# Fewer VectorE operations for the constants, and w_out as pairs of rows: a fused Nystrom attention and feed-forward kernel

## The chip, the cores and the metric

The kernel runs on one core of a Trainium2 chip. The metric is the device time of one execution in microseconds. A core has TensorE (PE in the profile; its weight loads are listed apart as PEld), VectorE (DVE), ScalarE (ACT), GpSimd (POOL) and SyncE (SP), each with its own queue of instructions that it takes in order, and 16 DMA engines that all queues share. Two notions matter below. A matmul has a loaded operand (the weights, put into TensorE by a weight load) and a moving operand that streams past it. And a group of TensorE results lies in PSUM until another engine copies it out.

## The reference

For 8 batches of 8 heads, 576 positions and 64 dimensions, the attention is Nystrom's: landmarks are means over groups of 18 positions, three softmax matrices are made with them, and the middle one is inverted by six iterations. The result goes through a feed-forward layer without a nonlinearity:

```python
A = sm(q, k_lm); Bm = sm(q_lm, k_lm); C = sm(q_lm, k)
Z = Bm.transpose(0, 1, 3, 2) / (norm1 * norminf + 1e-06)
for _ in range(6):
    Z = 2 * Z - Z @ Bm @ Z
x = A @ Z @ C @ v              # then (tokens, heads * dim): 4608 x 512
a = x @ w1                     # 512 x 1024
b = x @ w2
h = a * b @ w3                 # 1024 x 1024
out = h @ w_out                # 1024 x 512
```

All inputs and the output are fp32. Since nothing stands between w3 and w_out, the kernel multiplies these two first.

## The kernel before

All instructions are in an order written out by hand: each engine runs its own in the order in which the program states them. The string ORDER (line 32) lists the steps after the opening; a word such as `TK0.1` names a step and a batch, and `F` is one step of the fold.

The **opening** (lines 580 to 615) issues the first loads on the SyncE and ScalarE queues, starts some idle matmuls on TensorE (`warm_up`), has GpSimd copy one element of a late w_out block (`gate`, line 603) so that the q and k loads issued after it on GpSimd's queue wait for that block, issues those four loads and the loads of w1 and w2 (`load_weight`), builds the constants on VectorE (`constants`, line 162), and takes the first step of the fold.

The **fold** (line 505) makes w34 = w3 @ w_out, 1024 x 512. For precision each factor is split in two fp16 parts, a high and a low one, after a scaling by 256, and three of the four products are summed. `split(c)` does that for a block of 128 rows of w_out: ScalarE makes the high part, VectorE the low part. `turn(j, cc)` turns half a block of w3: TensorE transposes four pieces of 128 x 128 (line 517, moving operand the identity, loaded operand the piece of w3f) into a PSUM tile `big`, then ScalarE and VectorE split it into `w3t` (lines 522 and 523). `product(j, c)` is three matmuls of 512 columns into one accumulator (line 530); after eight of them ScalarE copies the block of w34 out (line 533). `before` and `order` in `fold` say which split and which turn stand ahead of which product: 64 products, 16 turns and 8 splits. After the first steps, blocks of w3 are used in turn out of three buffers, and the attention's first steps stand between the steps of the fold.

The **attention** of a batch takes q and k through 32 x 32 transposes on VectorE (`TK`, `TQ`, line 143), sums landmarks (`SK`, `SQ`), and makes scores (lines 248, 274, 322) from the tile `lm`, in which neighbouring landmarks of one head pair lie eight fp16 apart. The inverse runs in six steps (`I`, line 399). Constants are used there: `mask4` in the norms and in the inverse, `eye`, `eye2`, `bt`, `onesq` in the denominators (line 362), `selc` in the normalisation (line 382). Then `project` (`G`, line 442), `up` (`U`, line 455) and `down` (`W`, line 495) do the feed-forward layer.

Of the kernel before, what the change touches and what calls it, by code (L numbers as in the profile page):

```python
# [14 lines left out]
B = 8  # L15
H = 8
S = 576
D = 64
# [10 lines left out]
WS = 256.0  # L29
CHAINS = ((0,), (1, 2), (3, 4), (5, 6), (7,))  # L30

ORDER = """
F F F F F F F F F F F F F TK0.0 F F F F F TQ0.0 TQ1.0 F F L3.3 F TK1.0 F F F F F SK0.0 SK1.0 F F
SQ0.0 P.4 F F F F L3.5 F L3.7 F F TQ0.1 TK0.1 SQ1.0 F F L3.6 TK1.1 F E.0 F B.0 F C0.0 SK0.1 N.0
F F F A0.0 R.0 FV.0 TQ1.1 F SK1.1 F I0.0 F F D.0 I1.0 F I2.0 Y0.0 Y1.0 SQ0.1 Y2.0 LK0.2 F X.0 F
I3.0 LK1.2 F F F I4.0 V0.0 V1.0 SQ1.1 LQ0.2 LQ1.2 E.1 F LK0.3 TK0.2 TK1.2 F LK1.3 I5.0 F V2.0
LV0.2 F TQ0.2 TQ1.2 A0.1 Z.0 SK0.2 LV0.1 LV1.1 F M0.0 LV2.1 F LV3.1 D.1 Y0.1 Y1.1 Y2.1 G0.0 G1.0
G2.0 M1.0 SK1.2 F SQ0.2 TK0.3 G3.0 TK1.3 C0.1 X.1 F F F F U0a.0 U0b.0 U1a.0 U1b.0 U2a.0 U2b.0
LQ0.3 TQ0.3 LQ1.3 LK0.4 U3a.0 LV1.2 V0.1 U3b.0 SQ1.2 E.2 U4a.0 U4b.0 B.1 U5a.0 U5b.0 N.1 V1.1
SK0.3 V2.1 R.1 U6a.0 U6b.0 TQ1.3 U7a.0 I0.1 M0.1 LK1.4 LQ0.4 U7b.0 W0.0 SK1.3 I1.1 W1.0 I2.1  # L40
A0.2 LV2.2 TK0.4 LV3.2 W0.1 I3.1 TK1.4 W1.1 I4.1 M1.1 LQ1.4 W0.2 TQ0.4 I5.1 W1.2 SQ0.3 SQ1.3
TQ1.4 Z.1 SK0.4 E.3 SK1.4 SQ0.4 LV0.3 C0.2 G0.1 D.2 G1.1 G2.1 W0.3 Y0.2 G3.1 V0.2 V1.2 Y1.2 V2.2
LV0.4 Y2.2 U0a.1 U0b.1 LV1.3 LK0.5 U1a.1 U1b.1 LV1.4 LK1.5 X.2 U2a.1 U2b.1 U3a.1 U3b.1 Z.2 SQ1.4
E.4 U4a.1 U4b.1 U5a.1 G0.2 TK0.5 U5b.1 U6a.1 U6b.1 M0.2 LQ0.5 LQ1.5 W1.3 U7a.1 LV2.3 U7b.1 LV3.3
M1.2 W0.4 G1.2 G2.2 G3.2 B.3 TK1.5 W1.4 U0a.2 A0.3 W0.5 U0b.2 U1a.2 LV2.4 D.3 Y0.3 Y1.3 SK0.5
U1b.2 Y2.3 C0.3 W1.5 LK0.6 U2a.2 U2b.2 U3a.2 W0.6 X.3 U3b.2 U4a.2 N.3 SK1.5 V0.3 V1.3 V2.3 R.3
U4b.2 TK0.6 W1.6 LV3.4 U5a.2 U5b.2 W0.7 TQ0.5 U6a.2 I0.3 M0.3 LK1.6 TQ1.5 W1.7 I1.3 SQ0.5 LQ0.6
U6b.2 W0.8 I2.3 W1.8 I3.3 U7a.2 U7b.2 W0.9 I4.3 M1.3 W1.9 I5.3 A0.4 LQ1.6 Z.3 C0.4 W0.10 G0.3
G1.3 G2.3 D.4 W1.10 Y0.4 LV0.5 SQ1.5 G3.3 E.5 LV1.5 U0a.3 U0b.3 Y1.4 W0.11 TK1.6 Y2.4 U1a.3
U1b.3 U2a.3 U2b.3 LK0.7 X.4 TK0.7 W1.11 TQ0.6 U3a.3 U3b.3 U4a.3 V0.4 V1.4 V2.4 SK0.6 SK1.6 A0.5  # L50
TQ1.6 W0.12 U4b.3 LV2.5 U5a.3 LV3.5 LK1.7 SQ0.6 U5b.3 Z.4 U6a.3 U6b.3 LV0.6 LV1.6 U7a.3 U7b.3
W1.12 M0.4 M1.4 G0.4 W0.13 SQ1.6 E.6 TK1.7 G1.4 G2.4 G3.4 SK0.7 W1.13 D.5 Y0.5 LQ0.7 Y1.5 Y2.5
C0.5 U0a.4 X.5 W0.14 SK1.7 W1.14 U0b.4 U1a.4 U1b.4 B.5 V0.5 V1.5 V2.5 U2a.4 U2b.4 N.5 W0.15
U3a.4 U3b.4 W1.15 A0.6 TQ0.7 R.5 M0.5 W0.16 U4a.4 I0.5 U4b.4 U5a.4 I1.5 U5b.4 U6a.4 I2.5 LV0.7
LQ1.7 TQ1.7 SQ0.7 SQ1.7 W1.16 I3.5 U6b.4 U7a.4 I4.5 M1.5 U7b.4 I5.5 LV2.6 LV1.7 LV3.6 W0.17 Z.5
C0.6 E.7 W1.17 D.6 G0.5 G1.5 G2.5 W0.18 Y0.6 Y1.6 G3.5 Y2.6 U0a.5 U0b.5 X.6 W1.18 U1a.5 U1b.5
U2a.5 B.7 V0.6 V1.6 V2.6 U2b.5 U3a.5 N.7 U3b.5 W0.19 U4a.5 U4b.5 U5a.5 U5b.5 Z.6 U6a.5 W1.19
LV2.7 G0.6 G1.6 G2.6 LV3.7 R.7 W0.20 A0.7 I0.7 W1.20 U6b.5 M0.6 M1.6 W0.21 U7a.5 G3.6 D.7 I1.7
U7b.5 W1.21 U0a.6 U0b.6 Y0.7 U1a.6 Y1.7 U1b.6 W0.22 W1.22 C0.7 U2a.6 W0.23 U2b.6 U3a.6 Y2.7
U3b.6 W1.23 V0.7 V1.7 V2.7 X.7 I2.7 U4a.6 W0.24 U4b.6 I3.7 U5a.6 W1.24 I4.7 U5b.6 U6a.6 I5.7  # L60
W0.25 Z.7 U6b.6 W1.25 M0.7 M1.7 G0.7 W0.26 U7a.6 U7b.6 W1.26 G1.7 G2.7 G3.7 W0.27 U0a.7 U0b.7
W1.27 U1a.7 U1b.7 W0.28 U2a.7 U2b.7 W1.28 U3a.7 U3b.7 U4a.7 W0.29 W1.29 U4b.7 U5a.7 U5b.7 W0.30
U6a.7 U6b.7 U7a.7 W1.30 U7b.7 W0.31 W1.31 W0.32 W1.32 W0.33 W1.33 W0.34 W1.34 W0.35 W1.35
# [4 lines left out]
def kernel(  # L68
# [66 lines left out]
    def load_weight(t, w):  # L135
        for qd in range(2):
            nc.gpsimd.dma_start(out=wup[64 * qd:64 * qd + 64, :, t, :],
                                in_=w[256 * qd:256 * qd + 256, :].rearrange("(h d) j -> d h j", d=D))
# [23 lines left out]
    def constants():  # L162
# [16 lines left out]
        nc.vector.memset(selc, 0.0)  # L179
# [3 lines left out]
        for c in range(4):  # L183
            sl = slice(32 * c, 32 * c + 32)
            for qd in range(2):
# [7 lines left out]
        for i in range(4):  # L193
            nc.vector.tensor_copy(out=bt[:, i, 32:64], in_=eye[:, 0])
# [310 lines left out]
    def fold(pf, wof, w3f, wsp, warm_up):  # L505
        turned, psW = {}, {}

        def split(c):
            hi, lo = wsp[:, 0, c, :], wsp[:, 1, c, :]
            nc.scalar.activation(out=hi, in_=wof[c], func=AXF.Copy, scale=WS)  # L510
            nc.vector.scalar_tensor_tensor(out=lo, in0=wof[c], scalar=WS, in1=hi,
                                           op0=ALU.mult, op1=ALU.subtract)

        def turn(j, cc):
            pst = big()
            for c4 in range(4):
                nc.tensor.transpose(out=pst[:, 0, 128 * c4:128 * c4 + 128],  # L517
                                    in_=w3f[j][:, 512 * cc + 128 * c4:512 * cc + 128 * c4 + 128],
                                    identity=ident[:, :])
            w3t = turned[j, cc] = pf.tile([128, 2, 4, 128], FP16, name="w3t", bufs=4)  # L520
            hi, lo = (w3t[:, i].rearrange("p c j -> p (c j)") for i in range(2))
            nc.scalar.activation(out=hi, in_=pst[:, 0, :], func=AXF.Copy, scale=WS)  # L522
            nc.vector.scalar_tensor_tensor(out=lo, in0=pst[:, 0, :], scalar=WS, in1=hi,  # L523
                                           op0=ALU.mult, op1=ALU.subtract)
# [10 lines left out]

        before = {0: [(split, 0), (turn, 0, 0), (warm_up, 3), (split, 1), (turn, 1, 0), (warm_up, 2)],
# [4 lines left out]
        for j in range(2, 8):  # L541
            before[8 * j] = [(turn, j, 1)]
            before[8 * j + 5] = [(turn, j + 1, 0)] if j < 7 else []
# [26 lines left out]
    def load_w3(j, cc=None, eng=nc.sync):  # L570
# [3 lines left out]
        eng.dma_start(out=w3f[j][:, sl], in_=moe_w3[128 * j:128 * (j + 1), sl])  # L574
# [131 lines left out]
```

## Time and profile before

| What | Value |
|---|---|
| Time, median of 3 runs | 263.89 us (263.86 to 265.2) |
| Profiled execution: time / span | 263.62 us / 261.8 us |
| TensorE busy | 251.5 us, 96% of the span |
| VectorE busy | 173.8 us, 66%, 352 instructions |
| ScalarE busy | 134.7 us, 51% |
| GpSimd busy | 103.2 us, 39% |
| Products of the fold, line 530 | 47.3 us busy |
| Transposes of w3, line 517 | 10.0 us busy, 64 matmuls |
| DMA | 37.78 MB in 25070 packets |

A matmul's end is modelled, so that neighbouring matmuls overlap in the busy times; the distance from the start of one group to the start of the next tells what it costs. In a line of groups the last parts are the busy time, the mean of one in ns, and the idle time ahead of it with what ended it. In a line of the time line the first number is the start, the second the length.

### The profile page before, as it was taken

Reading aid. Unit: us, or ns where it says so; the run is one execution under the profiler, and the core shown is the slowest. Engines: PE = TensorE matmul, PEld = TensorE weight load, DVE = VectorE, ACT = ScalarE, POOL = GpSimd, SP = SyncE. Lnnn points to the kernel's source line nnn. Section 1 sums busy time; section 2 is a strip of 40 time slices with the busy share of each in tenths; the row PEclk is TensorE's granted clock in tenths of the full one; section 3 lists DMA queues with packets and bytes.
Section 4 is the critical chain, followed back from the end, with each engine's and each line's share of the span. In section 5 each row is a group of like instructions: output and inputs, shape, how many; then the busy total and the mean of one; then the engine's idle time right before and its main releaser. Section 6 shows DMA issues by size and latency. Waiting matters only on the chain.

```text
span 261.8 us, 10518 instructions
## 1 busy us (share of the span) xinstructions
PE 251.5 (96%) x4578; PEld 148.7 (57%) x4578; DVE 173.8 (66%) x352; ACT 134.7 (51%) x305; POOL 103.2 (39%) x134
## 2 busy tenths in 40 slices
PE   7999999998989999999999999999999999999993
PEld 3455554454556558557654674766476556656642
DVE  8765887556958687788856958767775656464410
ACT  4543236343652565576449546746646555455531
POOL 3630018998981999027092597504400000000000
PEclk9999999999999999999999999999999999999999
DMA  6999998999963448976668496933640713222355
GB/s 236 333 243 284 245 248 191 183 137 240 175 105 50 120 101 167 216 195 114 131 100 162 101 214 150 161 58 86 147 86 3 173 43 80 45 62 61 81 118 127
DMA packets 25070, 37.78 MB, mean 144 GB/s; under 512 B 4672, under 2 KB 13120, under 8 KB 25024
## 3 DMA queue, kind: packets, MB, share of 16 engines
q1 hardware_dynamic: 14704, 24.65, 36.9%
q0 software_dynamic: 9728, 11.54, 28.1%
q10 hardware_dynamic: 592, 0.92, 1.1%
q8 instruction: 36, 0.59, 1.0%
q14 instruction: 10, 0.08, 0.1%
HBM read 38.80 MB, written 9.44 MB: 184 GB/s over the span
## 4 chain that ended last, share of the span: by engine, by line
PE 89%; DVE 4%; ACT 3%; issue 1%; DMA 1%; SPq 0%; DVEq 0%; ACTq 0%
PE big L455 23%; PE acc L495 22%; PE acc L530 14%; PE big L442 5%; PE big L344 5%; PE big L399 4%; PE big L517 2%; PE small L530 2%; PE big L382 2%; PE small L421 2%; PE big L274 1%; PE big L495 1%; PE big L322 1%; DVE ab L461 1%; PE small L248 1%
## 5 line engine op out<-in xcount | busy, mean ns | idle before, releaser
L455 PE MATMUL big<-ahat,gt 128*128 128x288 f16 x512 | 73.1, 287 | 0.7 <-DVE ab L461 0.6
L495 PE MATMUL acc<-w,ab 128*128 128x512 f16 x264 | 67.2, 380 | 0.0
L461 DVE TENSOR_TENSOR ab<-a_sb,big 128x576 f16<-128x576 f16 x64 | 48.0, 750 | 27.2 <-ACT a_sb L459 16.8
L455 PEld LDWEIGHTS <-gt 128*128 128x128 f16 x512 | 48.3, 98 | 21.1 <-issue 3.1
L459 ACT CAST a_sb<-big 128x576 f16<-128x576 f32 x64 | 40.8, 640 | 33.9 <-PE big L455 32.9
L206 POOL TENSOR_TENSOR tr<-qkT 128x1024 f32<-128x1024 f16 x14 | 29.7, 2123 | 70.0 <-DVE qkT L143 69.8
L530 PE MATMUL acc<-wsp,w3t 128*128 128x512 f16 x168 | 41.3, 380 | 0.7 <-ACT w L533 0.5
L495 PEld LDWEIGHTS <-ab 128*128 128x128 f16 x280 | 25.3, 98 | 24.9 <-issue 3.5
L499 ACT ACTIVATE o_sb<-acc 128x512 f32<-128x512 f32 x33 | 19.8, 599 | 19.5 <-PE acc L495 19.1
L530 PEld LDWEIGHTS <-w3t 128*128 128x128 f16 x192 | 18.1, 98 | 18.9 <-issue 1.3
L143 DVE STREAM_TRANSPOSE qkT<-qkn 128x576 uint32<-128x576 uint32 x32 | 24.0, 763 | 2.0 <-DMA qkn<-in_k_dram 2.0
L448 DVE TENSOR_SCALAR gt<-big 128x1024 f16<-128x1024 f32 x16 | 19.1, 1211 | 3.1 <-PE big L442 3.0
L446 ACT ACTIVATE gt<-big 128x1024 f16<-128x1024 f32 x16 | 15.9, 1032 | 5.9 <-PE big L442 5.9
L211 POOL TENSOR_TENSOR tr<-tr 128x512 f32<-128x512 f32 x14 | 17.9, 1282 | 0.6
L442 PE MATMUL big<-wup,zt 64*32 64x512 f16 x512 | 17.4, 380 | 0.2 <-ACT en L282 0.2
L523 DVE SCALAR_TENSOR_TENSOR w3t<-big,w3t 128x512 f16<-128x512 f32 x16 | 11.0, 687 | 10.0 <-ACT w3t L522 10.0
L522 ACT ACTIVATE w3t<-big 128x512 f16<-128x512 f32 x16 | 9.5, 596 | 13.9 <-PE big L517 13.8
L284 DVE STREAM_TRANSPOSE ent<-en 128x576 f32<-128x576 f32 x16 | 12.1, 768 | 4.4 <-ACT en L282 4.4
L344 PE MATMUL big<-vt,ent 64*32 64x64 f32 x1152 | 14.2, 226 | 0.0
L282 ACT ACTIVATE en<-big 128x288 f32<-128x288 f32 x32 | 12.7, 411 | 2.9 <-PE big L274 2.7
L344 PEld LDWEIGHTS big<-vt,ent 64*32 64x32 f32 x1152 | 12.7, 105 | 2.0 <-ACT a_sb L459 0.5
L328 ACT ACTIVATE eat<-big 128x576 f16<-128x576 f32 x16 | 9.6, 652 | 7.3 <-PE big L322 7.3
(214 smaller groups left out, 285.2 us busy)
## 6 DMA issues: line engine op xcount, KB each, us to landing
out_dram<-o_sb SPq DMA_DIRECT2D x70, 128.0 KB, 2.5
vt<-in_v_dram SPq DMA_DIRECT2D x16, 288.0 KB, 5.3
vt<-in_v_dram SPq DMA_DIRECT2D x32, 144.0 KB, 4.0
qkn<-in_k_dram POOLq DMA_DIRECT2D x12, 288.0 KB, 5.4
qkn<-in_q_dram POOLq DMA_DIRECT2D x12, 288.0 KB, 4.9
w3f<-in_moe_w_dram SPq DMA_DIRECT2D x6, 512.0 KB, 6.7
wup<-in_moe_w_dram POOLq DMA_DIRECT2D x4, 512.0 KB, 25.3
wof<-in_moe_w_out_dram SPq DMA_DIRECT2D x6, 256.0 KB, 4.5
```

The costliest lines, as they stand in the source:

```text
L143: nc.vector.transpose(out=st["qkT"][:, t, prs].rearrange("p c r q e -> p (c r q e)").bitcast(U32), in_=st["qkn"][:, t, prs, :].rearrange(" ...
L206: add(out=tr, in0=x[:, :, 0:4, :], in1=x[:, :, 4:8, :], op=ALU.add)
L211: add(out=tr[:, :, 0:2, :], in0=tr[:, :, 0:2, :], in1=tr[:, :, 2:4, :], op=ALU.add)
L344: nc.tensor.matmul(psV[32 * o:32 * o + 32, qd, 0:64], ent[sl, pr, r, :], vt[sl, pr, 64 * r:64 * r + 64], start=(r == 0), stop=(r == RT - 1 ...
L442: nc.tensor.matmul(psG[o:o + 32, qd, :], zt[rs, i, h, :], wup[rs, h, w, fs], start=(i == 0), stop=(i == 1), tile_position=(64 * qd, o))
L448: nc.vector.tensor_scalar(out=g[:, :, w, fs], in0=psG, scalar1=1.0 / ZS, scalar2=None, op0=ALU.mult)
L455: nc.tensor.matmul(p[:, c, 0:HS], st["g"][:, qd, w, 128 * j:128 * j + 128], st["ahat", qd][:, c, :], start=(qd == 0), stop=(qd == 1))
L459: nc.scalar.copy(out=st["a_sb"], in_=p[:, :, 0:HS])
L461: nc.vector.tensor_tensor(out=st["ab"][:, j, st["t0"]:st["t0"] + S].rearrange("p (c s) -> p c s", c=2), in0=st["a_sb"], in1=p[:, :, 0:HS], ...
L495: nc.tensor.matmul(pso[:, :], ab[:, j, t0:t0 + 128], w34[:, j, :], start=(j == 0), stop=(j == 7))
L499: nc.scalar.activation(out=o_sb, in_=pso, func=AXF.Copy, scale=1.0 / (X64 * X64))
L530: nc.tensor.matmul(psW[j][:, :], turned[j, c // 4][:, a, c % 4, :], wsp[:, b, c, :], start=(c == 0 and a + b == 0), stop=(c == 7 and a == 1))
```

## The change

Three things are changed, and the order of the steps otherwise stays.

1. **Constants.** `eye` is written for both halves by one copy with a repeated source (4 copies for 8). `onesq` is made by two operations from `mask4` where there were eight memsets. `selc` is made by two products over all 128 partitions where there were a memset and eight copies. `bt` takes one copy for four.
2. **w_out in pairs.** A tile `wof` holds two rows of w_out for each partition, neighbours in memory, so that a packet of such a load has 4 KB where it had 2 KB. There are four tiles, of which three can be held, for eight of which six can be held. The first pair is loaded in two halves, one on each queue. A block c of the contraction is now the rows 512h + 4p + n for h = c // 4, n = c % 4 and p from 0 to 127, instead of 128 neighbouring rows.
3. **w3 to match.** A piece of a turn takes the columns n, n + 4, n + 8, ... of its half of w3, 128 of them, instead of 128 neighbours.

`load_weight` is split into four words `LW` at the start of ORDER: it is written after the constants, the fold's first step and three loads on SyncE, and on GpSimd's queue it keeps its place. The gate reads the third pair. `TURN = 8` leaves a second way of turning, on VectorE, unused, and the word `WT` does not occur in ORDER.

```diff
+TURN = 8
-F F F F F F F F F F F F F TK0.0 ...
+LW.0 LW.1 LW.2 LW.3 F F F F F F F F F F F F F TK0.0 ...
...
         for h in range(4):
             sl = slice(32 * h, 32 * h + 32)
             nc.vector.memset(mask4[sl, h, :], 1.0)
-            for qd in range(2):
-                nc.vector.tensor_copy(out=eye[sl, qd, :], in_=ident[sl, sl])
-                nc.vector.memset(onesq[sl, qd, :, qd, h:h + 1], 1.0 / X64)
+            nc.vector.tensor_copy(out=eye[sl], in_=ident[sl, sl].unsqueeze(1).to_broadcast([32, 2, 32]))
+        for qd in range(2):
+            nc.vector.tensor_scalar(out=onesq[:, qd, :, qd, :],
+                                    in0=mask4[:, :, 0].unsqueeze(1).to_broadcast([128, 4, 4]),
+                                    scalar1=1.0 / X64, scalar2=None, op0=ALU.mult)
...
-        nc.vector.memset(selc, 0.0)
...
-        for c in range(4):
-            sl = slice(32 * c, 32 * c + 32)
-            for qd in range(2):
-                nc.vector.tensor_copy(
-                    out=selc[sl, qd, c, :].rearrange("p (h m) -> p h m", m=32),
-                    in_=selr[sl, 4 * qd:4 * qd + 4].unsqueeze(2).to_broadcast([32, 4, 32]),
-                )
+        for qd in range(2):
+            nc.vector.tensor_tensor(
+                out=selc[:, qd].rearrange("p c (h m) -> p c h m", m=32),
+                in0=selr[:, 4 * qd:4 * qd + 4].unsqueeze(1).unsqueeze(3).to_broadcast([128, 4, 4, 32]),
+                in1=mask4[:, :, 0].unsqueeze(2).unsqueeze(3).to_broadcast([128, 4, 4, 32]), op=ALU.mult)
...
-        for i in range(4):
-            nc.vector.tensor_copy(out=bt[:, i, 32:64], in_=eye[:, 0])
+        nc.vector.tensor_copy(out=bt[:, :, 32:64], in_=eye[:, 0].unsqueeze(1).to_broadcast([128, 4, 32]))
...
         def split(c):
             hi, lo = wsp[:, 0, c, :], wsp[:, 1, c, :]
-            nc.scalar.activation(out=hi, in_=wof[c], func=AXF.Copy, scale=WS)
+            wo = wof[c // 2][:, c % 2, :]
+            nc.scalar.activation(out=hi, in_=wo, func=AXF.Copy, scale=WS)
...
         def turn(j, cc):
...
-                                    in_=w3f[j][:, 512 * cc + 128 * c4:512 * cc + 128 * c4 + 128],
+                                        in_=w3f[j][:, 512 * cc + n:512 * cc + 512:4],
...
-    def load_wout(c, eng):
-        wof[c] = pf.tile([128, DM], FP32, name="wof", bufs=6)
-        eng.dma_start(out=wof[c], in_=moe_w_out[128 * c:128 * c + 128, :])
+    def load_wout(pr, eng, i=slice(0, 2)):
+        if pr not in wof:
+            wof[pr] = pf.tile([128, 2, DM], FP32, name="wof", bufs=3)
+        eng.dma_start(out=wof[pr][:, i, :],
+                      in_=moe_w_out.rearrange("(h p m i) f -> h m p i f", h=2, m=2, i=2)[pr // 2, pr % 2][:, i, :])
 
     load_w3(0, 0)
-    load_wout(0, nc.scalar)
+    load_wout(0, nc.scalar, slice(0, 1))
+    load_wout(0, nc.sync, slice(1, 2))
+    load_w3(1, 0, nc.scalar)
     load_wout(1, nc.sync)
-    load_w3(1, 0, nc.scalar)
-    load_wout(2, nc.sync)
     ready = consts.tile([128, 1], FP32, name="ready")
     nc.scalar.activation(out=ready, in_=ident[:, 0:1], func=AXF.Copy, scale=WS)
-    load_wout(3, nc.scalar)
     load_w3(0, 1)
-    load_wout(4, nc.sync)
+    load_wout(2, nc.sync)
     load_w3(1, 1)
-    load_wout(5, nc.sync)
...
-    nc.gpsimd.tensor_copy(out=gate, in_=wof[4][:, 0:1])
+    nc.gpsimd.tensor_copy(out=gate, in_=wof[2][:, 0, 0:1])
...
-    load_wout(6, nc.sync)
-    load_wout(7, nc.sync)
+    load_wout(3, nc.sync)
     load_w3(2)
```

More of the change, by code (lines that the diff above doesn't have):

```diff
@@ L38 @@
[L38 to L61, printed above, removed]
@@ L133, in load_v, with load_weight @@
                         in_=v[b].rearrange("h (e p r) d -> e p h (r d)", e=2, r=RT)[1 - ph][:, heads[i]])
-    def load_weight(t, w):
-        for qd in range(2):
-            nc.gpsimd.dma_start(out=wup[64 * qd:64 * qd + 64, :, t, :],
-                                in_=w[256 * qd:256 * qd + 256, :].rearrange("(h d) j -> d h j", d=D))
+    def load_weight(n):
+        t, qd = n // 2, n % 2
+        w = (moe_w1, moe_w2)[t]
+        nc.gpsimd.dma_start(out=wup[64 * qd:64 * qd + 64, :, t, :],
+                            in_=w[256 * qd:256 * qd + 256, :].rearrange("(h d) j -> d h j", d=D))
     def turn(st, t, prs):
@@ L534, in product @@
                                      scale=1.0 / (WS * WS))
+        hold["turn"] = turn
         before = {0: [(split, 0), (turn, 0, 0), (warm_up, 3), (split, 1), (turn, 1, 0), (warm_up, 2)],
@@ L541, in fold @@
         for j in range(2, 8):
-            before[8 * j] = [(turn, j, 1)]
-            before[8 * j + 5] = [(turn, j + 1, 0)] if j < 7 else []
+            before[8 * j] = [(turn, j, 1)] if j < TURN else []
+            before[8 * j + 5] = [(turn, j + 1, 0)] if j + 1 < TURN else []
             order += [(j, c) for c in range(8)]
@@ L607 @@
     load_qk(sts[1], 1, 0)
-    load_weight(0, moe_w1)
-    load_weight(1, moe_w2)
     mask4, eye, eye2, onesq, selc, lomask, bt, xsp = constants()
@@ L661 @@
             paced_w3(int(b))
+        elif name == "LW":
+            load_weight(int(b))
+        elif name == "WT":
+            hold["turn"](int(b) // 2, int(b) % 2)
         elif name == "L3":
```

70 lines of the change are left out of this document (54 added, 16 removed).

## The prediction

> **What bounds the kernel now.** I read the page's busy shares and its chain first, then the time line of the head, then the groups of weight loads with different shapes kept apart, then the DMA queues in short stretches. The sum below is against the profiled execution's own 263.62 us (span 261.8, 1.8 around it); the median of the three runs, 263.89, lies 0.27 above it. The page:
>
> ```profile
> PE 251.5 (96%) x4578; PEld 148.7 (57%) x4578; DVE 173.8 (66%) x352; ACT 134.7 (51%) x305; POOL 103.2 (39%) x134
> ...
> PE 89%; DVE 4%; ACT 3%; issue 1%; DMA 1%; SPq 0%; DVEq 0%; ACTq 0%
> ```
>
> TensorE is busy 96% of the span and is 89% of the chain that ended last. The page's granted clock is 9 tenths or more in all 40 slices. So a microsecond added to TensorE in the first 60 us, where the fold of w3 and w_out runs, is nearly a microsecond of the result; one taken from another engine counts only where TensorE waits for it. The time line shows where that is:
>
> ```profile
> 1.11 0.17 DVE L167 MEMSET mask<- 128x128 f32 x1
> ...
> 3.14 0.48 DVE L179 MEMSET selc<- 128x512 uint32 x1 [0.15 <-issue]
> ...
> 5.98 0.55 DVE L197 MEMSET xsp<- 128x256 f32 x2
> ...
> 6.44 0.63 DVE L511 SCALAR_TENSOR_TENSOR wsp<-wof,wsp 128x512 f16<-128x512 f32 x1
> ...
> 6.87 0.63 PE L530 MATMUL acc<-wsp,w3t 128*128 128x512 f16 x2
> ...
> 7.71 0.33 PEld L530 LDWEIGHTS <-w3t 128*128 128x128 f16 x3 [0.74 <-DVE w3t L523]
> ...
> 9.00 0.51 POOL L603 COPY gate<-wof 128x1 f32<-128x1 f32 x1 [5.79 <-DMA wof<-in_moe_w_out_dram]
> ```
>
> The constants hold VectorE from 1.11 to 6.5 us. Its first split then starts at 6.44, though ScalarE's half was ready at 5.34, and the third product matmul waits for VectorE at 7.7. The gate at 9.00 opens when w_out's fifth block has landed; the q and k loads are queued behind it.
>
> A little later:
>
> ```profile
> 17.39 0.60 PE L517 MATMUL big<-ident,w3f 128*128 128x128 f32 x4
> ...
> 17.66 0.78 DVE L143 STREAM_TRANSPOSE qkT<-qkn 128x576 uint32<-128x576 uint32 x1 [2.02 <-DMA qkn<-in_k_dram]
> ...
> 17.82 1.46 PE L530 MATMUL small<-wsp,w3t 128*128 128x512 f16 x6
> ...
> 18.70 0.69 DVE L523 SCALAR_TENSOR_TENSOR w3t<-big,w3t 128x512 f16<-128x512 f32 x1 [0.27 <-ACT w3t L522]
> ...
> 19.55 3.40 PE L530 MATMUL acc<-wsp,w3t 128*128 128x512 f16 x15
> ```
>
> Four transposes take 17.82 - 17.39 = 0.43 us from start to start, 0.108 each. And the weight loads, with their mean ns:
>
> ```profile
> L517 PEld LDWEIGHTS big<-ident,w3f 128*128 128x128 f32 x64 | 7.8, 144 | 3.8 <-issue 1.2 <-DMA w3f<-in_moe_w_dram 0.3
> L442 PEld LDWEIGHTS <-zt 64*32 64x32 f16 x512 | 6.0, 91 | 8.7 <-issue 4.1 <-ACT a_sb L459 0.7 <-ACT zt L426 0.2
> ...
> L322 PEld LDWEIGHTS <-lm 32*32 32x32 f16 x256 | 2.5, 134 | 1.9 <-issue 1.9
> L248 PEld LDWEIGHTS <-lm 32*32 32x32 f16 x128 | 2.3, 149 | 1.7 <-issue 1.1 <-ACT lm L226 0.5
> ...
> L362 PEld LDWEIGHTS <-onesq 128*32 128x32 f16 x64 | 1.0, 95 | 3.0 <-issue 3.0
> L399 PEld LDWEIGHTS big<-sz__2498,tz__2500 32*32 32x32 f32 x32 | 0.4, 104 | 0.2 <-issue 0.2
> ```
>
> zt, onesq and tz are read with neighbouring columns. lm is the one operand read with a step of 16 bytes (eight fp16). In the transpose w3f is the loaded operand, and its new step, four fp32, is 16 bytes too.
>
> **The constants.** Removed: 8 onesq memsets (62 ns), the memset of selc (485), 8 selc copies (1.45 us together), 8 eye copies and 4 bt copies (0.43 together). Added: 4 eye copies of 64 columns, 2 small onesq operations (as L182, about 0.15 each), 2 selc products of 128x512 in fp32 (as L211, 0.69 each), one bt copy (about 0.2). selc: 1.38 for 1.93; bt saves 0.2; the four blocks of mask, eye and onesq took 3.14 - 1.33 = 1.81 us and will take about 0.85, plus 0.3 for onesq. In all about 1.4 us less, so VectorE is free at about 5.1, before ScalarE's first half at 5.34. What this is worth on TensorE has a ceiling: from 6.87 to 19.55 it has 48 product matmuls at 0.215 (six take 1.29) and four turns at 0.43, 12.04 of 12.68 us. So at most 0.64 us is gained, the waits for VectorE; I take 0.6. Earlier than 6.87 it can't start: the second turn waits for its w3 half, which lands at 5.94 and is not moved.
>
> **w_out in pairs.** The DMA queue's packets carry twice the bytes for twice the time: from 7 to 9 us queue 1 moved 0.75 MB at 101% of the engines, 23 GB/s for each; from 15 to 18 us, nearly all in 4 KB packets, 0.52 MB at 46.3%, 23 GB/s again. So packets give nothing; bounds 0 to 0.2 us. Two issues fewer at the head lift the wait of 1.6 us that SyncE had before the second half of w3's block 1; TensorE wants that half at 12.4, so nothing. But the gate now waits for a pair of 512 KB that ends one 256 KB unit later, 0.26 MB / 385 GB/s = 0.68 us. POOL's queue behind it (four q and k loads, then four weight loads) moves with it, and k lands at up to 18.3. VectorE, in order, holds the split of turn (2,0) behind that transposition: 18.3 + 0.74 + 0.69 = 19.7, wanted at 19.55 + 0.43 = 19.98, less what TensorE gained. Alone it costs 0; beside the gain of 0.6 it takes up to 0.4 of it back. The later q and k blocks and the four w1/w2 loads (21 to 28 us to landing, first read at 63) have room. load_weight is written later, past the constants, the fold's first step and SyncE's three loads; on POOL it still follows the four q and k loads, so 0.
>
> **The step of four.** A contiguous fp32 load costs (144 - 104) / 96 columns = 0.42 ns a column, 53 for 128. A load of 32 lm columns is longer than a contiguous one by 30 (134 against 104) to 58 ns (149 against 91), that is 0.94 to 1.8 a column. If it goes by columns, 128 of them stream for 53 + 120 = 173 to 285 ns; I take the middle, 134 against 94, 1.25 a column, 213. If it is a fixed delay for each load, 83 to 111. The load runs beside the matmul ahead of it: fp32 moving columns cost (221 - 196) / 32 = 0.78 ns in L399 (64 and 32 columns), so the 128 of the identity account for the 0.108 by themselves, and the contiguous load is hidden. A load of 213 sticks out by 105 in three of four; the first of a turn lies beside a product matmul of 0.215 and is hidden. That is 0.315 a turn, 5.0 us in 16 turns, and 0.2 once in the first turn, which has nothing ahead. With 173: 3.1; with 285: 0.60 a turn, 9.6; with the fixed delay: 0.
>
> The row first: at a step of 16 bytes lm's loads are slower, while the qkT columns, read with a step of 4 bytes, cost little (316 ns for L274's 288 columns, 287 for L455's). [...]
>
> What takes something back: TensorE waits twice, 0.25 us each, at 26.0 and 32.5, straight after a turn, for ScalarE to free the accumulator (0.5 us in the waits). Longer turns fill that: -0.5. Sum: +5.0 + 0.2 - 0.6 - 0.5 = +4.1, so 263.6 + 4.1 = 267.7 us. Ends of this case: 3.1 + 0.1 - 0.6 - 0.4 = +2.2 (265.8) and 9.6 + 0.2 - 0.6 - 0.5 = +8.7 (272.3).
>
> **Rivals.**
> - Not slower: the strided load stays under the 0.108 of the identity's pass. It speaks for this that lm's excess may be a fixed delay, or come from four row groups loading at once. Against it: the excess grows to 58 where matmuls read lm as well. It decides at 108 ns for 128 columns. Then only the head counts, -0.6 plus up to 0.4: 263.0 to 263.4.
> - Much slower: loads of over 250 ns, since the matmul reads SBUF beside them, as in L248: 270 to 272.3.
> - Clearly faster: the hidden case, and the 1.27 us wait of L349 at 58.6, released by nothing that the profile shows, goes too: 263.6 - 0.6 - 1.3 = 261.7. TensorE's instructions there stay the same, so I see little reason.
>
> **How the numbers follow.** Forecast (265.8 to 270) 0.62, hidden 0.27, much slower 0.06, clearly faster 0.05. The likeliest gives 267.7. The range goes down to the hidden case, 263.0, and up to 270.5; the forecast's own is 265.8 to 270. This kernel's measurement tells about 0.5%, 1.3 us, from no change: slower 0.67 (a little of the forecast's low end may fall under 1.3), same 0.27, faster 0.06.
>
> **What would show it.** Right: weight loads of the turn at 260 to 340 ns instead of 144, four transposes at 0.7 us instead of 0.43, TensorE's first products without the wait for VectorE, its first split at 5.4, the gate near 9.7, k's transposition near 18.3. Wrong: loads under 200 ns and turns still of 0.43.

## The result: 0.7% slower, and the profile after

The changed kernel takes 266.24 us in the median of 10 runs (264.34 to 268.8), the kernel before, run beside it, 263.91 us (263.38 to 265.2). The ratio is 1.007, with a 95% interval of 1.0043 to 1.0096. The ratio compares means, and leaves out executions in a slower state that this chip has now and then, here the one of 268.8 us; by it the change costs about 1.85 us, by the medians 2.3. The profiled execution of the changed kernel is the fastest of its ten: 264.34 us, span 262.2, that is 0.72 us above the profiled execution of before. Its page shows the small end of the loss, and for the rest more executions are needed (experiment 1). From the page, the busy times and the chain:

```profile
PE 252.0 (96%) x4578; PEld 150.1 (57%) x4578; DVE 172.9 (66%) x332; ACT 134.7 (51%) x305; POOL 103.0 (39%) x134
...
PE 84%; DMA 7%; DVE 3%; ACT 3%; issue 1%; SPq 1%; POOL 0%; DVEq 0%; ACTq 0%; POOLq 0%
PE big L456 23%; PE acc L496 22%; PE acc L538 12%; PE big L443 5%; PE big L345 5%; PE big L400 3%; DMA qkn<-in_k_dram 3%; DMA wof<-in_moe_w_out_dram 3%; PE big L383 2%; DVE ab L462 2%; PE big L520 2%; PE small L422 2%; PE big L275 1%; PE big L496 1%; PE big L323 1%
```

TensorE has almost the same work (252.0 for 251.5 us), VectorE twenty instructions fewer. What is new is in the chain: DMA has 7% of it where it had 1%, and two names stand there, the load of k and the load of w_out. The reader should take two things from it: TensorE was not made much busier, so a large extra cost of the loads of weights is already unlikely; and the end of the kernel now hangs on two transfers of the first 20 us.

The line numbers have moved: the transposes of w3 are L520, the products of the fold L538, the splits of the turns L530 and L531, the gate L620, and k's transposition L146.

The loads of the turn, from the groups with different shapes kept apart:

```profile
L520 PEld LDWEIGHTS big<-ident,w3f 128*128 128x128 f32 x64 | 10.0, 205 | 3.3 <-issue 1.4 <-DMA w3f<-in_moe_w_dram 0.2
L249 PEld LDWEIGHTS <-lm 32*32 32x32 f16 x128 | 2.3, 148 | 1.7 <-issue 1.1 <-ACT lm L227 0.5
```

A load is 205 ns long, where it was 144 with neighbouring columns: 61 ns more for 128 columns. The head, from the time line of each engine:

```profile
2.87 1.49 PE L616 MATMUL big<-warm 128*128 128x512 f16 x3
4.90 0.99 PE L520 MATMUL big<-ident,w3f 128*128 128x128 f32 x4 [0.54 <-DMA w3f<-in_moe_w_dram]
...
7.28 1.46 PE L538 MATMUL acc<-wsp,w3t 128*128 128x512 f16 x6
```
```profile
4.77 0.55 DVE L198 MEMSET xsp<- 128x256 f32 x2
5.68 0.69 DVE L513 SCALAR_TENSOR_TENSOR wsp<-wof,wsp 128x512 f16<-128x512 f32 x1 [0.36 <-ACT wsp L512]
```
```profile
9.57 0.18 POOL L620 COPY gate<-wof 128x1 f32<-128x1 f32 x1 [6.36 <-DMA wof<-in_moe_w_out_dram]
10.12 0.91 POOL L109 DMA_DIRECT2D qkn<-in_k_dram  x1 [0.37 <-issue]
```

VectorE is through with the constants at 5.32 (4.77 + 0.55) where it was 6.53, its first split starts at 5.68 and not 6.44, and TensorE's first six products run without the wait of 7.7 us. But TensorE now has the first half block of w3 at 4.90, not 4.66: it idles 0.54 us for it, where it was 0.30. And from there to the warm-up products it takes 0.83 us (to 5.73), where it was 0.67, mostly because TensorE's slow stretch at the start (last section) ends later in this execution. The three together leave TensorE 0.17 us ahead of before at 8 us, not 0.6. The gate is the step to watch next. Around 20 us:

```profile
17.28 0.63 PE L520 MATMUL big<-ident,w3f 128*128 128x128 f32 x4
17.75 1.46 PE L538 MATMUL small<-wsp,w3t 128*128 128x512 f16 x6
...
19.52 0.59 PE L538 MATMUL acc<-wsp,w3t 128*128 128x512 f16 x2
20.31 2.98 PE L538 MATMUL acc<-wsp,w3t 128*128 128x512 f16 x13 [0.20 <-DVE w3t L531]
```
```profile
18.90 0.78 DVE L146 STREAM_TRANSPOSE qkT<-qkn 128x576 uint32<-128x576 uint32 x1 [3.39 <-DMA qkn<-in_k_dram]
19.60 1.45 DVE L531 SCALAR_TENSOR_TENSOR w3t<-big,w3t 128x512 f16<-128x512 f32 x2
```

Four transposes take 17.75 - 17.28 = 0.47 us from start to start, 0.04 more than the 0.43 of before. Over 16 turns that is about 0.6 us. VectorE waits 3.39 us for k, which comes at 18.90 (before: 17.66); the two splits of L531 stand behind it in VectorE's order, and TensorE waits 0.20 us for the first. That wait is counted from the modelled end of the product before it; from start to start the third product comes 0.36 us late (20.31, where 19.52 and two products of 0.215 give 19.95). From there TensorE is 0.33 us behind the kernel before, 0.63 at 48 us and 0.74 at 58. Then it is about 0.3 behind to the end, since a wait at 60 us that has no releaser in the profile is 0.86 us and not 1.27. (Such distances compare the starts of the same instruction of TensorE in two profiles.)

### The profile page after: what moved, and what is told of

It reads as the page before. It is cut to its first block, busy times and chain, and to the rows that moved or that the text cites. A ratio compares the mean times of both kernels' runs of the same rounds, so it can differ in the third digit from the quotient of the medians.

```text
span 262.2 us, 10491 instructions
## 1 busy us (share of the span) xinstructions
PE 252.0 (96%) x4578; PEld 150.1 (57%) x4578; DVE 172.9 (66%) x332; ACT 134.7 (51%) x305; POOL 103.0 (39%) x134
## 3 DMA queue, kind: packets, MB, share of 16 engines
HBM read 38.80 MB, written 9.44 MB: 184 GB/s over the span
## 4 chain that ended last, share of the span: by engine, by line
PE 84%; DMA 7%; DVE 3%; ACT 3%; issue 1%; SPq 1%; POOL 0%; DVEq 0%; ACTq 0%; POOLq 0%
PE big L456 23%; PE acc L496 22%; PE acc L538 12%; PE big L443 5%; PE big L345 5%; PE big L400 3%; DMA qkn<-in_k_dram 3%; DMA wof<-in_moe_w_out_dram 3%; PE big L383 2%; DVE ab L462 2%; PE big L520 2%; PE small L422 2%; PE big L275 1%; PE big L496 1%; PE big L323 1%
## 5 line engine op out<-in xcount | busy, mean ns | idle before, releaser
L538 PE MATMUL acc<-wsp,w3t 128*128 128x512 f16 x168 | 41.1, 379 | 0.6 <-ACT w L541 0.4
L538 PEld LDWEIGHTS <-w3t 128*128 128x128 f16 x192 | 18.3, 99 | 18.5 <-issue 1.0
L146 DVE STREAM_TRANSPOSE qkT<-qkn 128x576 uint32<-128x576 uint32 x32 | 24.0, 763 | 4.0 <-DMA qkn<-in_k_dram 3.4
L531 DVE SCALAR_TENSOR_TENSOR w3t<-big,w3t 128x512 f16<-128x512 f32 x16 | 11.0, 685 | 9.3 <-ACT w3t L530 9.2
L530 ACT ACTIVATE w3t<-big 128x512 f16<-128x512 f32 x16 | 9.5, 596 | 14.2 <-PE big L520 13.8
```

Of the source, the lines that this page charges most:

```text
L146: nc.vector.transpose(out=st["qkT"][:, t, prs].rearrange("p c r q e -> p (c r q e)").bitcast(U32), in_=st["qkn"][:, t, prs, :].rearrange(" ...
L538: nc.tensor.matmul(psW[j][:, :], turned[j, c // 4][:, a, c % 4, :], wsp[:, b, c, :], start=(c == 0 and a + b == 0), stop=(c == 7 and a == 1))
```

## Experiments

Each run stands beside runs of the kernel before on the same chip; ratios are to those, with 95% intervals. Runs 1 to 4 shared a chip, and so did 5 to 8, 9 to 11, and 13 to 15.

### 1. The changed kernel again

> The changed kernel once more, since its profiled execution (264.34 us) is at the low end of its ten runs (median 266.24). Theory A, late k: most of the loss is the q and k loads, which start after the gate and so land later; then a run near 266 shows k's transposition on VectorE later than the 18.9 us of the profile at hand, near 20.5, and a wait of TensorE for the split of turn (2,0) near 2 us in place of 0.2. Theory B, step of four: the loss is in the turns; then a run near 266 has weight loads well above the 205 ns of the profile at hand, near 300 ns.

265.79 us, ratio 1.0039 (1.0008 to 1.007). The profiled execution was the longest of its set, 266.93 us, and shows what the first did not:

```profile
20.27 0.78 DVE L146 STREAM_TRANSPOSE qkT<-qkn 128x576 uint32<-128x576 uint32 x1 [4.77 <-DMA qkn<-in_k_dram]
```
```profile
21.68 2.55 PE L538 MATMUL acc<-wsp,w3t 128*128 128x512 f16 x11 [1.57 <-DVE w3t L531]
```

The same program, the same gate (9.59), the same length of a load (205 ns), and k comes 1.4 us later than in the first profile. TensorE waits 1.57 us for VectorE and is 1.70 us behind the kernel before from there. This is about half of the 3.3 us by which this execution is longer than the profiled one of before, and it varies from one execution to the next. The turns add 0.5 us up to 58 us, and another 0.6 comes between 140 and 175 us, where a wait for the landing of lm is part of it; no edit is shown to be its cause.

### 2. The step of four alone

```diff
-        eng.dma_start(out=wof[c], in_=moe_w_out[128 * c:128 * c + 128, :])
+        eng.dma_start(out=wof[c], in_=moe_w_out.rearrange("(h p n) f -> h n p f", h=2, n=4)[c // 4, c % 4])
...
-                                     in_=w3f[j][:, 512 * cc + 128 * c4:512 * cc + 128 * c4 + 128],
+                                     in_=w3f[j][:, 512 * cc + c4:512 * cc + 512:4],
```

> The kernel before with the step of four alone: w_out in eight loads of 256 KB with 2 KB packets as before (rows 512h + 4p + n), gate and constants as before. A, late k: the gate is where it was, so k lands near 17.7; only the turns cost, 16 x 0.04 = 0.6 us, some of it filled by waits: 264.0 to 264.6. B, step of four: nearly the whole loss stays, 265.5 to 266.5.

264.99 us for 264.33 before: 1.0031 (1.0001 to 1.006), about 0.8 us. That lies between the two expectations, nearer to A. Its loads are those of the changed kernel:

```profile
L517 PEld LDWEIGHTS big<-ident,w3f 128*128 128x128 f32 x64 | 10.0, 205 | 3.3 <-issue 1.5
```

k is transposed at 18.81, not near 17.7, but without a wait of TensorE after it. So the step and the rows four apart cost under 1 us, and not 4 to 5. TensorE has the first half block of w3 at 4.96 here, late as in the changed kernel, although the packets are 2 KB: it is late with the rows four apart, and 4 KB packets are not needed for it.

### 3. The constants alone

The kernel before with the new function `constants`, of which this is a part:

```diff
-        for c in range(4):
-            sl = slice(32 * c, 32 * c + 32)
-            for qd in range(2):
-                nc.vector.tensor_copy(
-                    out=selc[sl, qd, c, :].rearrange("p (h m) -> p h m", m=32),
...
+        for qd in range(2):
+            nc.vector.tensor_tensor(
+                out=selc[:, qd].rearrange("p c (h m) -> p c h m", m=32),
```

> The kernel before with the new constants alone. Both theories: VectorE is free at 5.3 instead of 6.5, TensorE's wait at 7.7 goes, k lands near 17.7; 263.3 to 263.7, that is 0.2 to 0.6 us less than before.

264.28 us for 264.33: 0.9998 (0.9976 to 1.002). The 0.2 to 0.6 us that were expected are not to be seen in the time. In its profile TensorE's slow stretch lasted until about 6.9 us (last section), which hides what is saved there.

### 4. The gate on the second pair of w_out

```diff
-    nc.gpsimd.tensor_copy(out=gate, in_=wof[2][:, 0, 0:1])
+    nc.gpsimd.tensor_copy(out=gate, in_=wof[1][:, 0, 0:1])
```

> The changed kernel with the gate on the second pair of w_out instead of the third. A, late k: the q and k loads start 1.5 to 2 us earlier, k lands near 17 and TensorE does not wait for it: 263.6 to 264.3, if the q and k loads do not take so much of the DMA engines that the last w_out pair and w3 come late. B, step of four: still 266.

266.32 us in four runs, 1.0082 (1.0051 to 1.0112). The profile shows no wait for k (the gate opened at 7.89, k's transposition is at 18.40), and a load takes 207 ns, so the figure that B gave came without B's cause. TensorE was 2 us late at its first product: it ran its warm-up products, and then its first products too, at 0.43 us each until about 10 us. That is 2.0 of the 2.5 us by which it is behind at the end. One profile does not tell whether the gate does that; experiment 15 takes it up.

### 5. k's transposition three products later

```diff
-LW.0 LW.1 LW.2 LW.3 F F F F F F F F F F F F F TK0.0 F F F F F TQ0.0 ...
+LW.0 LW.1 LW.2 LW.3 F F F F F F F F F F F F F F F F TK0.0 F F TQ0.0 ...
```

> The changed kernel with VectorE's first transposition of k put three steps of the fold later, behind the splits of turns (2,0) and (2,1); nothing else is moved. Late k: TensorE no longer waits at 20 to 22 us however late k lands, and the runs lose their spread upward: median 264.2 to 264.9, few runs over 265.5. If the loss is in the turns or in the clock of the first microseconds: still 265.5 to 266.3.

265.28 us for 264.23, 1.0026 (0.9986 to 1.0066), profiled at 264.78. TensorE waits for nothing at 20 us, and is 0.08 us behind the kernel before at 23 us, 0.24 at 39, 0.40 at 52. The slow growth is the 0.04 us of each turn. At 60 us the wait without a releaser is longer than before and adds 0.3. The median lies between the two expectations, and has not come down by more than its interval allows.

### 6. Everything but the step of four

```diff
-                                         in_=w3f[j][:, 512 * cc + n:512 * cc + 512:4],
+                                         in_=w3f[j][:, 512 * cc + 128 * n:512 * cc + 128 * n + 128],
```

> The changed kernel with w3 turned in pieces of neighbouring columns again; w_out stays in pairs, so that rows and columns no longer belong together and the output is another product. Turns cost 0.43 us again and loads 144 ns: by the turns 0.6 us less than the changed kernel, 265.2 to 265.7; the first landing at 4.9 and k after 18.7 stay. If the step of four carries the whole loss: 263.5 to 264.

265.43 us for 264.23: 1.0053 (1.0026 to 1.0079). A load is back at 140 ns, and still the kernel is slower by as much as the changed one, within the intervals:

```profile
L520 PEld LDWEIGHTS big<-ident,w3f 128*128 128x128 f32 x64 | 7.6, 140 | 4.3 <-issue 1.5 <-DMA w3f<-in_moe_w_dram 0.6
```

```profile
20.20 0.78 DVE L146 STREAM_TRANSPOSE qkT<-qkn 128x576 uint32<-128x576 uint32 x1 [4.77 <-DMA qkn<-in_k_dram]
```
```profile
21.61 2.76 PE L538 MATMUL acc<-wsp,w3t 128*128 128x512 f16 x12 [1.68 <-DVE w3t L531]
```

With this the theory of the prediction falls: the loss is there without the longer loads. TensorE is 0.22 us ahead of the kernel before at 19.5 us, 1.64 behind after the wait for k, and still 1.64 at 58: the turns add nothing here, and the wait 1.86.

### 7. The changed kernel with the old constants

```diff
-            nc.vector.tensor_copy(out=eye[sl], in_=ident[sl, sl].unsqueeze(1).to_broadcast([32, 2, 32]))
+            for qd in range(2):
+                nc.vector.tensor_copy(out=eye[sl, qd, :], in_=ident[sl, sl])
+                nc.vector.memset(onesq[sl, qd, :, qd, h:h + 1], 1.0 / X64)
```

(and so for `selc` and `bt`)

> The changed kernel with the constants of before: w_out in pairs and the step of four alone. If k lands late, what the constants gain at 7.7 us is spent in the wait for k, so that this is no slower than the changed kernel: 265.7 to 266.3. If the constants' gain reaches the end, this is 0.6 us slower: 266.3 to 266.9.

265.78 us for 264.23: 1.0051 (1.0025 to 1.0077). k's transposition at 19.87, TensorE's wait 1.00 us. The new constants neither make the loss nor take a visible part of it.

### 8. The new constants, and k's transposition later

The kernel of experiment 3 with the order of experiment 5:

```diff
-F F F F F F F F F F F F F TK0.0 F F F F F TQ0.0 ...
+F F F F F F F F F F F F F F F F TK0.0 F F TQ0.0 ...
```

> The new constants alone, w_out and w3 as before, with k's first transposition three steps of the fold later: a candidate to beat both. Late k: 263.2 to 263.9 with few runs over 264.5. If k is no cause: as the constants alone, 264.3.

264.34 us for 264.23: 1.0 (0.998 to 1.002). Its profiled execution took 263.47 us; TensorE is 0.43 us ahead of before from 8 us on and keeps that to the end. This is the gain of the constants where TensorE's slow stretch ends early and w3 lands early; the median does not show it, and is the figure that was expected if k is no cause. But in its profile k landed at 16.1 us (the gate opened at 8.90), so that there was no late k to get out of the way, and the run says nothing for or against that cause.

### 9 to 11. Two warm-up products more

TensorE idles between its seventh warm-up product and the landing of w3. If the length of its slow stretch came from that idle time, two products more should end the spread.

```diff
-    warm_up(7)
+    warm_up(9)
```

In experiment 9 this goes with k's later transposition, in 10 it is alone; 11 is the kernel of experiment 8 with `warm_up(8)`.

> The changed kernel with k's first transposition three products later on VectorE, and nine warm-up products instead of seven, so that TensorE does not idle between the end of the warm-ups (4.36 us) and the landing of the first w3 half (4.90 to 4.97 us in every run with w_out's rows four apart). Theory: what is left of the loss after the late k is moved out of the way is the slow clock at the start, which lasts longer where TensorE idles 0.54 to 0.61 us there: products at the slow spacing of 0.43 us end by 5.3 us, and the runs, which with the later transposition alone went from 263.9 to 268.1, come together at 264.0 to 264.8, the median by 0.5 to 1.0 us below that kernel's 265.3. Rival: the idle stretch has nothing to do with the spread; the two products more then only delay the first transpositions by about 0.3 us (5.22 against 4.93), and the median is 265.3 to 265.6.

> The changed kernel with nine warm-up products instead of seven and nothing else. Theory of two causes: the slow clock ends by 5.3 us in every execution, the wait for k near 20 us stays (0.2 to 1.7 us, k's transposition at 18.9 to 20.3 us), and the median is 264.9 to 265.5, 0.3 to 0.9 below that of the changed kernel (265.8 to 266.2). Rival, the late k alone makes the loss: no gain, 266.0 to 266.4.

> The kernel before with the new constants, k's first transposition three products later, and eight warm-up products instead of seven (w_out and the columns as before). The eighth product ends at about 4.79 us, when the first w3 half has just landed (4.66 to 4.75). Theory: without the idle stretch of 0.3 us the clock is up by about 5 us every time, and what the constants save (0.4 us on TensorE after 8 us) shows in the time: 263.4 to 263.9, under the kernel before by 0.4 to 0.8. Rival: the length of the slow stretch is chance and does not follow the idle time; then 264.2 to 264.4, no difference from the kernel before, as with seven.

Measured beside the same runs of before (264.07 us): experiment 9 264.18 us, 1.0002 (0.998 to 1.0023); experiment 10 265.66 us, 1.0057 (1.0028 to 1.0086); experiment 11 264.28 us, 1.0003 (0.9974 to 1.0032). 9 came as its theory said. 10 and 11 did not gain; 11 is at its rival's figure, 10 between its two. The time line of TensorE after 5 us, of experiment 9 and then of 10:

```profile
5.01 0.98 PE L520 MATMUL big<-ident,w3f 128*128 128x128 f32 x4
5.82 0.81 PE L616 MATMUL big<-warm 128*128 128x512 f16 x3
6.47 0.63 PE L520 MATMUL big<-ident,w3f 128*128 128x128 f32 x4
```
```profile
5.00 1.06 PE L520 MATMUL big<-ident,w3f 128*128 128x128 f32 x4
5.86 1.43 PE L616 MATMUL big<-warm 128*128 128x512 f16 x3
7.13 0.64 PE L520 MATMUL big<-ident,w3f 128*128 128x128 f32 x4
```

Three warm-up products take 0.65 us in one and 1.27 in the other. The idle time is gone in both, so it does not decide how long the slow stretch lasts: that half of my theory falls. What stays is the pair itself. 9 and 10 differ in one thing, whether the split stands behind k, and by 265.66 - 264.18 = 1.48 us on one chip, with intervals that do not overlap. VectorE in experiment 9 takes the split first and loses nothing by a k that lands at 20.0:

```profile
18.70 0.69 DVE L531 SCALAR_TENSOR_TENSOR w3t<-big,w3t 128x512 f16<-128x512 f32 x1 [3.09 <-ACT w3t L530]
20.46 0.69 DVE L531 SCALAR_TENSOR_TENSOR w3t<-big,w3t 128x512 f16<-128x512 f32 x1 [1.07 <-ACT w3t L530]
21.07 0.77 DVE L146 STREAM_TRANSPOSE qkT<-qkn 128x576 uint32<-128x576 uint32 x1
```

Not all of the 1.48 us is seen in the two profiles, where TensorE in experiment 10 loses 0.46 us behind k (0.29 of it counted as a wait) and 0.66 to the longer slow stretch.

### 12. 2 KB packets again

```diff
-    load_wout(1, nc.sync)
+    load_wout(1, nc.sync, slice(0, 1))
+    load_wout(1, nc.sync, slice(1, 2))
...
-    nc.gpsimd.tensor_copy(out=gate, in_=wof[2][:, 0, 0:1])
+    nc.gpsimd.tensor_copy(out=gate, in_=wof[2][:, 1, 0:1])
```

(and the same for the third and fourth pair)

> The changed kernel with each 512 KB load of w_out cut in two of 256 KB, even and odd rows of the pairs, so that no w_out packet is longer than 2 KB; rows, columns, constants and the gate (which waits for the second half of the third pair) are as in the changed kernel. It asks what makes k late: in the profiles so far, k's first load takes from its issue to its landing 8.1, 9.0, 9.1, 6.7 and 7.5 us with w_out in 2 KB packets, and 8.1 to 10.1 us, 9.5 in the mean of eight, with 4 KB packets. If the packets' size does it: 7 to 9 us, k's first transposition at 17.5 to 19.0 us, a wait of TensorE for VectorE of at most 0.3 us near 20 us, and a median of 264.5 to 265.3. If it is the later gate, or the order of rows: 9.5 to 10 us, the transposition at 19.6 to 20.3, a wait of 0.5 to 1.7 us, and 265.6 to 266.2 as the changed kernel.

266.69 us for 264.22: 1.0087 (1.0058 to 1.0117). The profiled execution, 268.87 us, is the longest of its six. The gate opened at 10.10, k took 9.8 us from its issue, and TensorE waited longest of all:

```profile
20.48 0.78 DVE L146 STREAM_TRANSPOSE qkT<-qkn 128x576 uint32<-128x576 uint32 x1 [4.95 <-DMA qkn<-in_k_dram]
```
```profile
21.89 2.33 PE L538 MATMUL acc<-wsp,w3t 128*128 128x512 f16 x10 [1.76 <-DVE w3t L531]
```

TensorE is 1.9 us behind from there and 5.0 at the end. Of the rest, 0.8 goes to the wait without a releaser, which is 2.03 us here (60.9 to 63.0), and 1.5 to what follows it: the granted clock is 0.58 in the microsecond from 63 us and 0.50 in the two after it (0.989 in the mean of the execution). So k is as late with packets of 2 KB, and long packets of w_out are not what makes it late. The gate opened later still in this kernel, and that led to the next three.

### 13. The kernel before with the gate on the next tile

```diff
-    nc.gpsimd.tensor_copy(out=gate, in_=wof[4][:, 0:1])
+    nc.gpsimd.tensor_copy(out=gate, in_=wof[5][:, 0:1])
```

> The kernel before with one edit: the gate reads w_out's sixth tile instead of the fifth, so it opens one 256 KB unit later, as in the changed kernel (near 9.6 us instead of 9.0). Rows, packets, columns and constants are as before. If the gate makes k late: k is issued at about 10.1, takes 9.5 to 10 us (8.1, 9.0, 6.7, 7.5 with the gate at 8.8 to 9.0), lands near 19.7, TensorE waits 0.5 to 1.5 us for VectorE near 21 us, and the median is 0.8 to 1.5 us above the kernel before, 265.0 to 265.7. If it is the order of the rows: k takes 7 to 9 us and lands by 18.8, no wait, and the median stays within 0.4 us of the kernel before.

Old rows, old packets, old columns, old constants; and the wait is there. SyncE loads half a block of w3 between the two tiles, so the gate opens not one unit of 256 KB later but two: 1.21 us (10.21 for 9.00), twice the 0.57 of the changed kernel.

```profile
10.21 0.18 POOL L603 COPY gate<-wof 128x1 f32<-128x1 f32 x1 [7.01 <-DMA wof<-in_moe_w_out_dram]
```
```profile
19.65 0.78 DVE L143 STREAM_TRANSPOSE qkT<-qkn 128x576 uint32<-128x576 uint32 x1 [4.00 <-DMA qkn<-in_k_dram]
```
```profile
21.07 2.98 PE L530 MATMUL acc<-wsp,w3t 128*128 128x512 f16 x13 [0.91 <-DVE w3t L523]
```

k's transposition comes 2.0 us later than in the profile of before: 1.2 by its issue, 0.8 by a longer transfer (8.9 for 8.1 us, not the 9.5 to 10 that were expected). TensorE waits 0.91 us and is 1.09 us behind from there; the profiled execution is 264.71 us, 1.09 above that of before. The median, 265.05 for 264.64 us, ratio 1.0017 (0.9983 to 1.005), does not settle the size.

### 14. Experiment 12 with the gate on the first half

```diff
-    nc.gpsimd.tensor_copy(out=gate, in_=wof[2][:, 1, 0:1])
+    nc.gpsimd.tensor_copy(out=gate, in_=wof[2][:, 0, 0:1])
```

> The kernel of the halves (the changed kernel with w_out in 256 KB loads of 2 KB packets) with the gate reading the first half of the third pair, the fifth 256 KB unit as in the kernel before: it opens near 9.4 instead of 10.1 us. If the gate makes k late: k's transposition falls from 20.5 to 17.7 to 18.9 us, TensorE does not wait near 20 us, and the median falls from 266.7 by 1.0 to 2.0 us, to 264.7 to 265.7. If it is the order of the rows: the transposition stays at 19.6 or later, the wait at 0.5 us or more, and the median at 266.0 or more.

The gate opens at 9.44, k's transposition falls from 20.48 to 18.80, and of TensorE's wait of 1.76 us a delay of 0.2 is left in this profile (264.36 us). The median, 265.92 us, 1.0038 (1.0007 to 1.0069), fell less than it should have by the theory, and lies between the two expectations: with k at 18.8 the kernel stands at the edge, and other executions may be over it, which is not shown.

### 15. The changed kernel with the early gate, in more runs

> The changed kernel with the gate on the second pair of w_out rows, again and in more runs: it opens near 7.9 us. The first look had k at 18.4 and no wait, but a slow start of TensorE's clock (products 2 us late before 9 us), and four runs at 265.8 to 266.6. If the late k makes most of the loss and that start was chance: no wait near 20 us, and a median of 264.5 to 265.3. If an earlier k only moves the loss to the loads that it competes with: 265.7 to 266.6 again, with the products of the first 10 us late again.

264.67 us for 264.64: 1.001 (0.9982 to 1.0038). The gate opens at 7.83, the transposition is at 18.81, TensorE loses 0.08 us behind it, its products start at 7.48 us. So this gate does not always bring the slow start of experiment 4. The same kernel stood at 1.0082 in four runs there and at 1.001 in twelve here, on another chip: sets of runs can differ by more than their intervals tell, and a single ratio below is to be read with that in mind.

## Why the prediction was right and wrong

The time fell between the two main cases: right that it is slower, 1.85 us instead of 4.1. The forecast's own range, 265.8 to 270, just holds the median, but by luck: the term that it rested on was eight times too large, and a part of the loss came from one that its sum leaves out.

**The step of four: the term that failed.** I took 213 ns for a load to stream, 5.0 us in 16 turns. Measured: a load of 205 ns in all where 144 stood, four transposes in 0.47 us where 0.43 stood, so about 0.6 us, and 0.54 by the distances in the profile after. The prediction's own marks of being right were "260 to 340 ns" and "0.7 us"; neither came. Its marks of being wrong, "under 200 ns" and "0.43", were just missed too. The wrong choice was to stretch a row: lm's loads, of 32 columns and fp16, were taken to 128 columns of fp32 by 1.25 ns a column. By 61 ns over 128 columns the extra is 0.48 ns a column, about as much as a contiguous fp32 column costs (0.42). A load therefore streams in 53 + 61 = about 114 ns, an estimate from these rows, which sticks out from the 108 of the identity by so little that a turn grows by 0.04. Nearer to it was the prediction's other reading of lm's rows, a fixed delay of 30 to 58 ns for each load, so 83 to 111 ns: the 61 ns are just above the 58. Whether they are fixed or go by columns is not shown, since w3f was loaded with this step at 128 columns alone. Experiment 6 shows from the other side that this term does not make most of the loss: without the step the time was about the same.

**The gate and k: the second term, named, but far too small.** The prediction saw that the gate moves 0.68 us (near 9.7; it came at 9.57), that k follows, and that VectorE holds the split of turn (2,0) behind k's transposition. It put k at "up to 18.3" and the cost at "up to 0.4", and the sum has no term for it. Over the profiles, in two groups by when the gate opened; the time to landing is from the issue of k's first load:

| Kernel | gate us | k issued us | to landing us | TensorE's wait us |
|---|---|---|---|---|
| before | 9.00 | 9.54 | 8.1 | 0 |
| 2, step alone | 9.14 | 9.69 | 9.1 | 0 |
| 3, constants alone | 8.81 | 9.42 | 9.0 | 0 |
| 8, constants, k later | 8.90 | 9.45 | 6.7 | moved away |
| 11, the same, 8 warm-ups | 9.07 | 9.61 | 7.5 | moved away |
| 14, halves, early gate | 9.44 | 9.99 | 8.8 | 0 |
| 15, early gate | 7.83 | 8.37 | 10.4 | 0 |
| 4, early gate | 7.89 | 8.44 | 9.9 | 0 |
| after | 9.57 | 10.12 | 8.8 | 0.20 |
| 1, after again | 9.59 | 10.13 | 10.1 | 1.57 |
| 6, no step | 9.62 | 10.16 | 10.0 | 1.68 |
| 7, old constants | 9.64 | 10.19 | 9.7 | 1.00 |
| 10, 9 warm-ups | 9.58 | 10.13 | 9.6 | 0.29 |
| 5, k later | 9.61 | 10.16 | 8.1 | moved away |
| 9, k later, 9 warm-ups | 9.61 | 10.16 | 9.9 | moved away |
| 13, before with late gate | 10.21 | 10.76 | 8.9 | 0.91 |
| 12, halves | 10.10 | 10.64 | 9.8 | 1.76 |

From start to start each wait costs about 0.16 us more than the table says, and experiments 14 and 15 lose 0.20 and 0.08 us that are not counted as waits. Where the gate opened by 9.44, k landed by 18.8 in all eight profiles and TensorE lost 0.2 us at most. Where it opened at 9.57 or later, k landed at 18.3 to 20.5, past 19.6 in seven of nine, and TensorE waited in each of the seven profiles whose split stands behind k. Experiment 13 shows that a later gate does it without the other edits, though with twice the delay; 12 shows that packets of 4 KB are not needed, 14 and 15 that with an earlier gate the wait is nearly gone from the profile, 5 and 9 that it goes when the split no longer stands behind k.

How much of the time it is: 1.48 us between experiments 10 and 9, 0.4 to 1.9 us from start to start in single profiles. The medians do not all follow: experiments 4 and 14, with hardly a wait in their profiles, are still at 1.0082 and 1.0038, so the share of the wait in the loss of the median is not settled. What stays open, too, is why k loses more than the gate's 0.6 us, and why an issue at 8.4 us gains almost nothing (10.4 us to landing). The order of rows may have a part in it: with the gate at 8.8 to 9.14, k landed at 16.1 to 18.4 in the four profiles with neighbouring rows and at 18.8 in experiment 2. The prediction moved k's landing with its issue, one for one; the transfers don't do that here.

**The constants.** VectorE is free at 5.32 (said: about 5.1), the first split starts at 5.68 (5.4), the wait at 7.7 is gone. The gain of 0.6 was about right where nothing else moved (0.43 us in experiment 8, 0.53 in 11) and came out as 0.17 in the changed kernel, because TensorE has its first half block of w3 0.24 us later and its slow stretch ended later. I had let w3's landings stay. In the medians of experiments 3, 8 and 11 nothing of it is left to be seen.

**What would be taken back.** The 0.5 us in ScalarE's accumulator waits presumed long turns; with 0.04 a turn there was little to absorb, and 0.4 of them are left.

**The sum after the fact.** In the profile of 264.34 us, -0.17 at the head, +0.36 behind k and +0.54 in the turns make the 0.74 us that TensorE is behind at 58 us; then the shorter wait at 60 us gives 0.4 back. Of the 0.72 us in the time, 0.4 lie in the span and 0.3 around it. In that of experiment 1, -0.17 at the head, +1.7 behind k and +0.6 in the turns make 2.2 at 58 us, and some 0.8 comes after that, by waits that no edit is shown to cause. The mean loss of 1.85 us lies between the two. Of the rivals, "not slower" had the right turn (nearly hidden), and failed on k; "much slower" and "clearly faster" had nothing.

No kernel of these is faster than the kernel before: the constants with k's transposition later, at 1.0 and 1.0003, equals it.

## What to carry to other kernels

A tile made larger for its transfers also makes coarser everything that waits on it (here the gate opened at 9.57 us, where it was 9.00): ask of each gate which unit it waited for before, and what is queued behind it in an order that does not bend. An in-order engine that waits for a load with other work behind it needs more slack than a few tenths of a microsecond: k's landing differed by 1.4 us between two profiles of the same program. And a price stretched from a row of another size and type is no more than a guess; where two readings of that row lie 100 ns apart, as the 213 by columns and the 111 of a fixed delay do here, one direct measurement of the load is the cheapest thing to have.

## What the runs showed of the hardware

- A weight load of 128 fp32 columns at a step of 16 bytes takes 205 ns where neighbouring columns take 144 (140 in experiment 6). By the estimate above that is a stream of 114 ns for 53, and it almost hides behind 128 fp32 columns of a matmul: four transposes take 0.47 us for 0.43.
- The first loads come later when rows four apart are read: TensorE has the first half block of w3 at 4.90 to 5.13 us in the kernels of that order, where it waits for it, and at 4.66 to 4.75 in those with neighbouring rows. Between 2 and 4 us the DMA moved 221 to 266 GB/s in the twelve profiles of that order (239 in the changed kernel) and 266 to 300 in the five others (300 before). That the order does it with the old packets too, experiment 2 shows; why was not tried.
- TensorE starts with a product of 512 columns every 0.43 us, and goes over to 0.215 at some time between 4.8 us (experiment 8) and about 10 us (experiment 4). This makes up to 2 us of difference, is not tied to any edit here, and the granted clock in the profile is 1.00 all the while (in each microsecond up to 10 us in experiment 4; 1.000 in the mean of experiment 10). What the expectations call a slow clock is this spacing of 0.43 us; that a clock makes it is not shown. The length changes between profiles of the same kernel: the stretch lasts until about 10 us in experiment 4 and ends before 5.7 in experiment 15. No run shows what sets it.
